# More warm-up products, filler products among the first heads, and one reciprocal for two heads

## The chip, the cores and the metric

The kernel runs on one core of one Trainium2 chip. The metric is the device time of one execution in microseconds (us); less is better. Times given as a result are medians of several runs. A profile is one execution taken by the hardware profiler, with the time of every instruction on the five engines: PE (TensorE), DVE (VectorE), ACT (ScalarE), POOL (GpSimd) and SP (SyncE, which issues the DMAs).

## What is computed

A causal attention with a decay runs for 4 batches of 8 heads, 576 positions and head size 64; its output (2304 tokens of 512 features) goes through two feed-forward layers of 512 to 2048 to 512.

```python
scores = scale * np.matmul(q, k.transpose(0, 1, 3, 2))
cum = np.cumsum(np.log(np.clip(f, 0.0001, 1.0)), axis=-1)
scores = np.where(causal, -1e9, scores + cum[:, :, :, None] - cum[:, :, None, :])
attn = np.exp(scores - np.max(scores, axis=-1, keepdims=True))
attn = attn / (np.sum(attn, axis=-1, keepdims=True) + 1e-09)
x = np.matmul(attn, v)                       # then heads side by side, 512 features
x = np.square(np.maximum(x @ w_in, 0)) @ w_out
h = x @ w_in2
out = np.where(h >= 1, h, np.where(h <= -1, 0, (h + 1) ** 2 / 4)) @ w_out2
```

## The kernel before, in words

The tokens are cut into five blocks of up to 512. Block 0 holds the first 256 positions of batches 0 and 1. For a block the kernel needs its attention first, then 16 steps of the first feed-forward layer (`mo` 0) and 16 of the second. One step is 12 products `h` (L1016) of 128x512, the activation, and 12 products `acc` (L1067 to L1069). Weights come as 64-bit words, one pair of slices per step; in the first 32 steps DVE, ACT and POOL decode them (`wf`, `low`; the last add of a decode is L957 on DVE or L958 on POOL), split them into a high and a low part (`whl`: the high part on ACT, L990, or on DVE, L991; the low part on DVE, L993), and SP stores the split form for the later blocks.

The first 256 positions of all heads are done by `attention32` in eight groups of four heads; block 0 takes groups 0 to 3. A head has its scores on PE (`s0q` for group 0; the contraction has 66 rows, 64 features and two rows of the decay), a masked row maximum on DVE (L587, `E`), two exponentials with sums on ACT (L647), a small add and a reciprocal of the two sums on DVE (L652 and L653, tile `st`), two multiplications by the reciprocal on ACT, DVE or POOL (L661 to L663), three transposes on PE (`tr`, L669), a copy (`pr`), and for each two heads the products with the values (`av`, L683). Block 0's feed-forward steps start on PE when the first of these are in `x`.

Before all this `warm_up` issues 11 products of the 128x128 identity with itself, which no result uses (L542, tile `warm`).

No order is written out by hand. Every operation goes to a planner (`Schedule`) with a cost on each engine that could do it, a due time, what it depends on, and the buffers it holds from a ring; `improve` plans the whole program once for each of seven weightings of DVE and POOL work (`WEIGHTS`), keeps the plan with the shortest total, and `emit` writes the instructions in planned order. So a small edit can move instructions, and move work between engines, in the whole program. At run time each engine goes through its own list in order. SP issues all loads and stores in one list, and a load of a group's queries and keys (L603, two buffers `QK`) waits there until the scores of the group two before are done.

Of the kernel before, what the change touches and what calls it, by code (L numbers as in the profile page):

```python
# [8 lines left out]
F32 = mybir.dt.float32  # L9
# [7 lines left out]
AF = mybir.ActivationFunctionType  # L17
ALU = mybir.AluOpType
# [4 lines left out]
P = 128  # L23
# [9 lines left out]
CHUNKS = [(HEAD, 320), (320, 448), (448, S)]  # L33
# [14 lines left out]
QUAD = 4  # L48
SPARE = ("E", "g", "E", "o", "E", "r", "E", "g", "E", "o")

SLAV = [0.0, 0.51, 0.75, 0.75, 0.0]
# [2 lines left out]
VE = [5.5, 6.1]  # L54
RE = [1.36, 7.73, 16.0]
LW = 29.1
WARM = 11


def pattern(bits):  # L60
# [320 lines left out]
def tile_attention_moe_moe(ctx: ExitStack, tc: tile.TileContext, qkv, f, w2, outT):  # L381
    nc = tc.nc
    PSUM = bass.MemoryType.PSUM
    W64 = w2.dtype == U64
    sch = Schedule()
# [4 lines left out]
    def ring(tag, n, shape, dt, space=None, fifo=True, most=()):  # L390
        kw = {"space": space} if space else {}
        tp = ctx.enter_context(tc.tile_pool(name="p_" + tag, bufs=n, **kw))
        pools[tag] = (Pool(n, fifo, most), tp, shape, dt)

    def new(tag, name, shape=None, dt=None, kind=None):
        p, tp, sh, d = pools[tag]
        shape = sh if shape is None else shape
        kw = {"padded_shape": sh} if list(shape) != list(sh) and len(shape) == len(sh) and dt is None else {}
        return Buf(p, lambda: tp.tile(shape, dt or d, tag=tag, name=name, **kw), kind)
# [3 lines left out]
    ring("K1", 2, [P, S], F32R)  # L403
    ring("vt", 3, [P, 5, 2, 64], F32R)
    ring("E", 5, [P, S], F32)
    ring("st", 4, [P, 3, len(CHUNKS)], F32)
    ring("mm", 3, [P, 2], F32)
    ring("PP", 3, [P, (2 * NK - 1) * P], F16)
    ring("PT", 2, [P, QUAD * 4 * HEAD], F16)
# [31 lines left out]
    for s in range(NS):  # L441
        g, att = s // NFC, 0.0
# [90 lines left out]
    cum_op, zs, mask_op, id_op, cumd_op, first_rows = setup()  # L533
    xb = {0: new("x", "x0")}

    def warm_up():

        ps = new("ps", "warm")

        def mms(n):  # L540
            for _ in range(n):
                nc.tensor.matmul(ps.tile[:, :P], ident, ident, start=True, stop=True)  # L542

        sch.op(-90, {"PE": (0.43 * WARM, lambda: mms(WARM))}, [id_op], [ps])
# [46 lines left out]
    def attention32(g):  # L591

        first = g.blk == 0
        qk, n = QK[g.i % 2], QUAD * 2 * HEAD
# [6 lines left out]
        for i in range(parts):  # L601
            c = slice(n // parts * i, n // parts * (i + 1))
# [17 lines left out]
        vt = new("vt", f"vt{g.i}q")  # L620
# [5 lines left out]
            in_=qkv[g.at_v:g.at_v + P * vn].rearrange("(p n) -> p n", p=P)))}, [], [vt], early=VE[g.i] if g.i < len(VE) else g.due - 4)  # L626
        g.qk = []
        chunks = [(0, 0, P), (1, P, HEAD)]
        for c in range(QUAD):
            nm = f"{g.i}q{c}"  # L630
            t0 = g.due + g.len * c / QUAD
            a = c % 2
            Eb = new(SPARE[len(used) % len(SPARE)] if first else "E", f"E{nm}", [P, 3 * P])
            used.append(Eb)
            st = new("st", f"st{nm}")
            ps = new("acc" if first else "ps", f"s{nm}", kind="att")
            cols = lambda ci: slice(0, P) if ci == 0 else slice(P, 3 * P)
            o_e = []
            for ci, qa, e in chunks:
                o_s = sch.op(t0, {"PE": (4 * e / 2400, lambda c=c, ci=ci, qa=qa, e=e, ps=ps: nc.tensor.matmul(  # L640
                    ps.tile[:, cols(ci)], qr(c)[:, qa:qa + P], kr(c)[:, :e], start=True, stop=True))},
                    ready[c], [ps, Eb, qk])
                g.qk.append(o_s)
                o_t = sch.op(t0 + 0.3, {"DVE": (dve_t(e) + 0.01, lambda ci=ci, qa=qa, e=e, Eb=Eb, ps=ps, st=st: top(
                    Eb.tile[:, cols(ci)], ps.tile[:, cols(ci)], qa, e, P, -0.125, st.tile[:, 0, ci:ci + 1]))},
                    [o_s, mask_op[0]], [ps, Eb, st])
                o_e.append(sch.op(t0 + 0.8, {"ACT": (act_t(e, ptr=1) + 0.09, lambda ci=ci, Eb=Eb, st=st: nc.scalar.activation(  # L647
                    Eb.tile[:, cols(ci)], Eb.tile[:, cols(ci)], AF.Exp, scale=-1.0, bias=st.tile[:, 0, ci:ci + 1],
                    accum_out=st.tile[:, 1, ci:ci + 1]))}, [o_t], [Eb, st]))

            def recip(st=st):
                nc.vector.tensor_scalar(st.tile[:, 1, :2], st.tile[:, 1, :2], 1e-9, None, op0=ALU.add)  # L652
                nc.vector.reciprocal(st.tile[:, 2, :2], st.tile[:, 1, :2])  # L653

            o_r = sch.op(t0 + 2, {"DVE": (0.30, recip, True)}, o_e, [st])
            o_n = []
            for ci, qa, e in chunks:
                x = lambda ci=ci, Eb=Eb: Eb.tile[:, cols(ci)]
                r = lambda ci=ci, st=st: st.tile[:, 2, ci:ci + 1]
                o_n.append(sch.op(t0 + 2.5, {  # L660
                    "ACT": (act_t(e, ptr=1), lambda x=x, r=r: nc.scalar.activation(x(), x(), AF.Copy, scale=r())),  # L661
                    "DVE": (dve2_t(e), lambda x=x, r=r: nc.vector.tensor_scalar(x(), x(), r(), None, op0=ALU.mult), True),
                    "POOL": (pool_t(e), lambda x=x, r=r: nc.gpsimd.tensor_scalar(  # L663
                        x(), x(), r(), 0.0, op0=ALU.mult, op1=ALU.add)),
                }, [o_r], [Eb, st]))
            if a == 0:
                pr = new("pr", f"pr{nm}")
            tr = new("acc" if first else "ps", f"tr{nm}", kind="att")
            got = [sch.op(t0 + 3, {"PE": (0.11, lambda tr=tr, Eb=Eb, to=to, at=at: nc.tensor.transpose(  # L669
                tr.tile[:, to:to + P], Eb.tile[:, at:at + P], ident))}, [o_n[at > 0], id_op], [Eb, tr, pr])  # L670
                for to, at in ((0, 0), (P, P), (2 * P, 2 * P))]
            o_c = sch.op(t0 + 3.5, copies(
                lambda pr=pr, a=a: pr.tile[:, a, :3 * P].bitcast(F32), lambda tr=tr: tr.tile[:, :3 * P], 3 * P,
                "ACT DVE", psum=True), got, [tr, pr])
            if a == 0:
                o_c0 = o_c
                continue
            av = new("acc" if first else "ps", f"av{nm}", kind="att")
            o_m = None
            for kc in range(HEAD // P):  # L680
                def mms(c=c, kc=kc, pr=pr, av=av):
                    for i in range(2):
                        nc.tensor.matmul(  # L683
                            av.tile[D * i:D * i + D, kc * P:HEAD], v32(c - 1 + i, kc),
                            pr.tile[:, i, 2 * P * kc:2 * P * kc + HEAD - kc * P].bitcast(F32),
                            start=(kc == 0), stop=(kc == HEAD // P - 1))

                o_m = sch.op(t0 + 4, {"PE": (4 * (HEAD - kc * P) / 2400 + 0.05, mms)},
                             [o_c, o_c0, o_v, o_m], [av, vt, pr], SLAV[g.blk])
            x = xb[g.blk]  # L690
            kc = (g.h + c) // 2
            hi = lambda kc=kc: x.tile[:, kc, 0, g.off:g.off + HEAD]
            o3 = sch.op(t0 + 5, copies(hi, lambda av=av: av.tile[:, :HEAD], HEAD, "ACT DVE", psum=True), [o_m], [av, x])
            xops.setdefault((g.blk, kc), []).append(sch.op(t0 + 5.5, {
                "DVE": (dve_t(HEAD), lambda kc=kc, hi=hi, av=av: nc.vector.tensor_tensor(
                    x.tile[:, kc, 1, g.off:g.off + HEAD], av.tile[:, :HEAD], hi().bitcast(F32), op=ALU.subtract))},
                [o3], [av, x]))

    def attention(t):
        g, W, nm, due = t.b * H + t.h, REST, t.name, t.due  # L700
        unit = 1.0 / PS
# [6 lines left out]
        a = t.h % 2  # L708
# [36 lines left out]
        E, o_e = [], []  # L745
        for ci, (qa, e) in enumerate(CHUNKS):
# [8 lines left out]
            for pi, (s0, s1) in enumerate(pieces):  # L755
# [25 lines left out]

        def recip():
            nc.vector.tensor_scalar(
                st.tile[:, 1, :], st.tile[:, 1, :], 1e-9, unit, op0=ALU.add, op1=ALU.mult)
            nc.vector.reciprocal(st.tile[:, 2, :], st.tile[:, 1, :])  # L785

        o_r = sch.op(back(9.5), {"DVE": (0.30, recip, True)}, o_e, [st])

# [410 lines left out]
```

## Time and profile before

| | |
|---|---|
| runs | 956.57, 958.58, 959.28 us; median 958.58 us |
| the profiled execution | 955.24 us, of which 953.5 us is the span that the profile shows |
| busy in the span | PE 939.9, ACT 638.0, DVE 583.2, POOL 191.3 us |
| mean granted clock of TensorE | 0.989 |

Busy time of an engine is the time in which it had an instruction running. A clock of 1.00 is TensorE's 2.4 GHz, 0.50 is 1.2 GHz. Where no clock is on record, as at the very start, the profile prints 1.00.

### The profile page before, as it was taken

How to read it: one execution, taken by the hardware profiler on the slowest of the kernel's cores; microseconds unless marked ns; L12 is line 12 of the kernel's file. 1: busy time of each engine (PE TensorE's matmuls, PEld its weight loads, DVE VectorE, ACT ScalarE, POOL GpSimd, SP SyncE). 2: the span in 40 equal slices, each digit the busy share in tenths (PEclk: the TensorE clock that was granted, in tenths of full speed). 3: DMA queues.
4: the chain of work that ended last, by engine and by line, in shares of the span. 5: the costliest groups of instructions: out<-in, count | busy, mean ns of one | idle time of the engine just before them, and what ended most of it. 6: DMA issues, size and time to landing. Idle time of an engine off the chain costs nothing.

```text
span 953.5 us, 14248 instructions
## 1 busy us (share of the span) xinstructions
PE 939.9 (99%) x4758; PEld 789.2 (83%) x4758; DVE 583.2 (61%) x1325; ACT 638.0 (67%) x1269; POOL 191.3 (20%) x341
## 2 busy tenths in 40 slices
PE   8999999999999999999999999999999999999998
PEld 6777777777778888888888888788888888889998
DVE  6899999989757668777767667866311132220032
ACT  5999879997877768787777677686432343334454
POOL 3321010134122323342323124231000000002200
PEclk6999999999999999999999999999999999999999
DMA  6699998996998987898899988796665655659994
GB/s 192 207 337 402 339 403 292 369 347 227 349 321 246 277 247 251 231 285 248 242 257 287 253 261 238 208 300 186 248 232 178 202 194 181 207 189 374 365 374 143
DMA packets 126106, 254.73 MB, mean 267 GB/s; under 512 B 89808, under 2 KB 90480, under 8 KB 104080
## 3 DMA queue, kind: packets, MB, share of 16 engines
q1 hardware_dynamic: 126032, 253.81, 81.0%
q8 instruction: 38, 0.62, 0.3%
q14 instruction: 36, 0.29, 0.1%
HBM read 194.35 MB, written 38.45 MB: 244 GB/s over the span
## 4 chain that ended last, share of the span: by engine, by line
PE 90%; DVE 4%; DMA 4%; issue 1%; ACT 1%; SPq 0%; POOL 0%; DVEq 0%; ACTq 0%
PE h L1016 39%; PE acc L1067 13%; PE acc L1069 13%; PE acc L1068 13%; PE av L840 4%; PE s L761 2%; PE s L762 2%; DMA PT<-PP 2%; DMA in<-in_qkv_dram 1%; DMA out_dram<-o 1%; PE s1q L640 1%; DVE whl L993 0%; DVE wf L957 0%; PE s0q L640 0%; DVE low L942 0%
## 5 line engine op out<-in xcount | busy, mean ns | idle before, releaser
L1016 PE MATMUL h<-x,whl 128*128 128x512 f32 (+1 forms) x1896 | 432.5, 371 | 0.6 <-DVE whl L993 0.5
L1016 PEld LDWEIGHTS h<-x,whl 128*128 128x128 f32 x1896 | 325.7, 189 | 55.4 <-issue 2.1
L1067 PE MATMUL acc<-gh,whl 128*128 128x512 f32 (+1 forms) x640 | 240.1, 375 | 2.9 <-DVE o L571 2.9
L1069 PE MATMUL acc<-gl,whl 128*128 128x512 f32 (+1 forms) x640 | 237.2, 371 | 0.0
L1068 PE MATMUL acc<-gh,whl 128*128 128x512 f32 (+1 forms) x640 | 236.7, 370 | 0.0
L580 DVE TENSOR_TENSOR gl<-g,gh 128x512 fp32r<-128x512 f32 (+1 forms) x126 | 83.6, 663 | 120.1 <-PE acc L1069 81.5
L1069 PEld LDWEIGHTS acc<-gl,whl 128*128 128x128 f32 x640 | 121.0, 189 | 21.5 <-POOL gl L582 0.2
L1067 PEld LDWEIGHTS acc<-gh,whl 128*128 128x128 f32 x640 | 120.9, 189 | 20.9 <-DVE o L571 3.4
L1068 PEld LDWEIGHTS acc<-gh,whl 128*128 128x128 f32 x640 | 121.0, 189 | 15.7
L1034 ACT ACTIVATE r<-h 128x512 f32<-128x512 f32 (+1 forms) x80 | 44.0, 550 | 91.3 <-PE h L1016 82.6
L1047 DVE SCALAR_TENSOR_TENSOR g<-r,h 128x512 f32<-128x512 f32 (+1 forms) x80 | 50.4, 630 | 80.1 <-ACT r L1045 79.6
L582 POOL TENSOR_TENSOR gl<-g,gh 128x512 fp32r<-128x512 f32 (+1 forms) x34 | 39.7, 1169 | 287.3 <-PE acc L1069 213.6
L1043 ACT ACTIVATE r<-h,half 128x512 f32<-128x512 f32 (+1 forms) x80 | 51.1, 639 | 61.9 <-PE h L1016 61.6
L815 DVE SCALAR_TENSOR_TENSOR PP<-E,st,PP 128x512 f16<-128x512 f32 (+2 forms) x128 | 77.6, 638 | 11.0 <-ACT PP L811 10.1
L778 ACT ACTIVATE E<-E,st 64x320 f32<-64x320 f32 (+2 forms) x96 | 63.6, 662 | 24.1 <-DVE st L587 15.6
L587 DVE CUSTOM_DVE_ANT_0 E<-s,mask 128x288 f32<-128x288 f32 (+2 forms) x128 | 62.1, 502 | 28.3 <-PE s L762 20.1
L811 ACT ACTIVATE PP<-E,st 128x512 f16<-128x512 f32 (+2 forms) x128 | 68.9, 591 | 9.1 <-DVE st L785 7.7
L840 PEld LDWEIGHTS av<-pr,vt 128*128 128x128 f32 x288 | 53.9, 189 | 13.0 <-issue 1.7
L840 PE MATMUL av<-pr,vt 128*128 128x320 f32 (+2 forms) x288 | 61.8, 287 | 1.3 <-DVE pr L571 1.3
L568 ACT ACTIVATE gh<-g 128x512 fp32r<-128x512 f32 (+1 forms) x70 | 40.7, 581 | 31.5 <-DVE g L1047 31.1
L573 POOL TENSOR_SCALAR pr<-PT 128x640 fp32r<-128x640 f16 (+2 forms) x50 | 31.2, 627 | 108.4 <-PE av L840 57.3
L568 ACT ACTIVATE pr<-PT 128x640 fp32r<-128x640 f16 (+2 forms) x63 | 36.3, 580 | 18.2 <-DMA PT<-PP 11.8
(258 smaller groups left out, 1145.4 us busy)
## 6 DMA issues: line engine op xcount, KB each, us to landing
whl<-scr SPq DMA_DIRECT2D x112, 1024.0 KB
raw<-in_w_dram SPq DMA_DIRECT2D x28, 1024.0 KB
scr<-whl SPq DMA_DIRECT2D x28, 1024.0 KB
in<-in_qkv_dram SPq DMA_DIRECT2D x32, 608.0 KB
whl<-scr SPq DMA_DIRECT2D x32, 512.0 KB
out_dram<-o SPq DMA_DIRECT2D x16, 256.0 KB
QK<-in_qkv_dram SPq DMA_DIRECT2D x7, 512.0 KB
raw<-in_w_dram SPq DMA_DIRECT2D x6, 512.0 KB
```

Source lines behind the costliest of these rows:

```text
L568: alts["ACT"] = (act_t(n, psum), lambda: nc.scalar.activation(out(), in_(), AF.Copy))
L580: alts["DVE"] = (dve_t(n), lambda: nc.vector.tensor_sub(out(), a(), b()), True)
L587: return nc.vector.tensor_tensor_reduce(out=out, in0=ps, in1=mask[:m, OFF - q0:OFF - q0 + n], scale=scale, scalar=3e38, op0=ALU.add, op1=A ...
L778: nc.scalar.activation(Ec.tile[:m, :e], Ec.tile[:m, :e], AF.Exp, scale=-1.0, bias=nmx(), accum_out=st.tile[:m, 1, ci:ci + 1])))}, [*tops, ...
L811: nc.scalar.activation(hi, x, AF.Copy, scale=r())
L815: nc.vector.scalar_tensor_tensor(lo, x, r(), hi, op0=ALU.mult, op1=ALU.subtract)
L840: nc.tensor.matmul(av.tile[:, c0:W], vt.tile[:, kc, :, :], pr.tile[:, i, :n], start=(kc == 0 and i == 0), stop=(kc == NK - 1))
L1016: nc.tensor.matmul(ps.tile[:, :n], w.tile[:, 0, wi, kc * P:(kc + 1) * P], src.tile[:, kc, xi, :n], start=(kc == 0 and i == 0), stop=(kc == ...
L1043: o1 = sch.op(due, {"ACT": (act_t(n, True, 1), lambda: A.activation(r.tile[:, :n], ps(), AF.Relu, scale=0.5, bias=half))}, [o], [psb, r])
L1067: nc.tensor.matmul(a.tile[:, :n], wh, gh.tile[:, :n], start=(fc == 0), stop=False)
L1068: nc.tensor.matmul(a.tile[:, :n], wl, gh.tile[:, :n], start=False, stop=False)
L1069: nc.tensor.matmul(a.tile[:, :n], wh, gl.tile[:, :n], start=False, stop=(fc == NFC - 1))
```

## The change

`WARM` goes from 11 to 17. Fifteen more single products of the identity with itself are given to the planner as operations of their own, all on the buffer of the warm-up, with due time 900 (so that anything else that is ready goes first) and not before the planned times 9, 10, ... 23. In `attention32` the two heads of a pair now share one `st` tile with four sums, one add and one reciprocal, which wait for the exponentials of both; group 0 keeps a reciprocal for each head. The contraction of the scores stays at 66 rows.

```diff
-WARM = 11
+FILL, FILL_AT, FILL_STEP = 15, 9, 1
+WARM = 17
...
-    ring("st", 4, [P, 3, len(CHUNKS)], F32)
+    ring("st", 4, [P, 3, 4], F32)
...
         sch.op(-90, {"PE": (0.43 * WARM, lambda: mms(WARM))}, [id_op], [ps])
+        for i in range(FILL):
+            sch.op(900.0, {"PE": (0.22, lambda: mms(1))}, [id_op], [ps], early=FILL_AT + FILL_STEP * i)
...
+        def recips(c, st, n, deps):
+            def recip():
+                nc.vector.tensor_scalar(st.tile[:, 1, :n], st.tile[:, 1, :n], 1e-9, None, op0=ALU.add)
+                nc.vector.reciprocal(st.tile[:, 2, :n], st.tile[:, 1, :n])
+
+            return sch.op(g.due + g.len * c / QUAD + 2, {"DVE": (0.30, recip, True)}, deps, [st])
...
+        for c in range(0, QUAD, 2):
+            got = []
+            if g.i == 0:
+                for a in range(2):
+                    st = new("st", f"st{g.i}q{c + a}")
+                    Eb, o_e = exps(c + a, st, 0)
+                    got.append(probabilities(c + a, st, 0, Eb, recips(c + a, st, 2, o_e)))
+            else:
+                st = new("st", f"st{g.i}q{c}")
+                (E0, o0), (E1, o1) = (exps(c + a, st, 2 * a) for a in range(2))
+                o_r = recips(c + 1, st, 4, [*o0, *o1])
+                got = [probabilities(c + a, st, 2 * a, Eb, o_r) for a, Eb in enumerate((E0, E1))]
+            products(c + 1, got)
```

What PE finds at the start of its list, before the change (`s0q` and `s1q` are scores of groups 0 and 1, `tr` transposes):

```order
L542 MATMUL warm<-ident 128x128 x11
L640 MATMUL s0q_248<-QK_180 128x128
L640 MATMUL s0q_248<-QK_180 128x256
...
L640 MATMUL s0q_274<-QK_180 128x128
L669 MATMUL tr0q_295<-ident,E0q_249 128x128 x3
L640 MATMUL s1q_307<-QK_212 128x128
L669 MATMUL tr0q_312<-ident,E0q_256 128x128 x3
L640 MATMUL s1q_307<-QK_212 128x256
```

And with it, at the same place:

```order
L543 MATMUL warm<-ident 128x128 x17
L644 MATMUL s0q_255<-QK_180 128x128
L644 MATMUL s0q_255<-QK_180 128x256
...
L644 MATMUL s0q_283<-QK_180 128x256
L543 MATMUL warm<-ident 128x128 x3
L683 MATMUL tr0q_304<-ident,E0q_256 128x128 x3
L543 MATMUL warm<-ident 128x128
L644 MATMUL s1q_314<-QK_218 128x128
L644 MATMUL s1q_314<-QK_218 128x256
```

Three filler products now stand between the scores of group 0 and its first transpose, and one behind it; three more follow up to the first transposes of group 1, and eight behind that point.

DVE's list for two heads of group 1 before, from the maximum of the second head on:

```order
L587 ISA E1q_323,st1q_332<-s1q_322,mask 128x128
L587 ISA st1q_332 128x1
L587 ISA E1q_323,st1q_332<-s1q_322,mask 128x256
L587 ISA st1q_332 128x1
...
L652 TENSOR_SCALAR st1q_316<-st1q_316 128x2
L653 RECIPROCAL st1q_316<-st1q_316 128x2
...
L652 TENSOR_SCALAR st1q_332<-st1q_332 128x2
L653 RECIPROCAL st1q_332<-st1q_332 128x2
```

And with the change, the same two heads:

```order
L590 ISA E1q_334,st1q_324<-s1q_333,mask 128x256
L590 ISA st1q_324 128x1
...
L658 TENSOR_SCALAR st1q_324<-st1q_324 128x4
L659 RECIPROCAL st1q_324<-st1q_324 128x4
L675 TENSOR_SCALAR E1q_315<-E1q_315,st1q_324 128x256
L675 TENSOR_SCALAR E1q_334<-E1q_334,st1q_324 128x128
```

One pair of small instructions is left of two, and both heads' multiplications stand behind it.

## Rows read from the trace of the kernel before

**Rows 1.** The page: busy time of PE, and the clock in 40 slices.
```profile
PE 939.9 (99%) x4758; PEld 789.2 (83%) x4758; DVE 583.2 (61%) x1325; ACT 638.0 (67%) x1269; POOL 191.3 (20%) x341
...
PEclk6999999999999999999999999999999999999999
```

**Rows 2.** What PE waited for in all, before and after 70 us (two answers).
```profile
PE s0q L640 <- DMA QK<-setup: 2.9, 1, 2.9
...
PE acc L1067 <- DVE o L571: 2.9, 1, 2.9
```

**Rows 3.** Windows by stage: length, busy of PE, PEld, DVE, ACT, POOL, clock, DMA, GB/s.
```profile
6.00:8.84 2.84, 0.00 (x0) 0.03 (x1) 2.31 (x6) 1.39 (x2) 0.92 (x4) 0.98 0.50 111
8.84:25.81 16.97, 16.73 (x59) 12.65 (x61) 9.45 (x53) 9.62 (x36) 1.68 (x4) 0.50 0.66 203
25.81:36.10 10.29, 10.13 (x74) 6.99 (x70) 9.07 (x49) 9.17 (x34) 3.77 (x7) 1.00 0.66 150
36.10:46.00 9.90, 9.78 (x70) 7.65 (x69) 9.30 (x42) 9.71 (x28) 3.73 (x7) 1.00 0.84 307
46.00:246.00 200.00, 199.32 (x932) 157.31 (x931) 190.07 (x334) 179.12 (x297) 37.02 (x34) 1.00 0.92 339
```

**Rows 4.** PE in half-microseconds: length, busy, clock, DMA, GB/s.
```profile
8.50:9.00 0.50, 0.16 (x1) 0.74 0.48 147
9.00:9.50 0.50, 0.50 (x3) 0.50 0.88 295
...
25.50:26.00 0.50, 0.50 (x8) 0.69 1.83 246
```

**Rows 5.** The warm-up's products: nanoseconds shortest/median/longest, first and last start.
```profile
L542 PE MATMUL warm<-ident x22: 274/421/579, 1.4 to 5.7; 128*128 128x128 f32 x22
```

**Rows 6.** PE in order of time: start, length, idle before and its releaser.
```profile
1.39 4.59 PE L542 MATMUL warm<-ident 128*128 128x128 f32 x22 [1.39 <-POOL tiny L482]
8.84 5.46 PE L640 MATMUL s0q<-QK 66*128 66x128 f32 x16 [2.86 <-DMA QK<-setup]
...
19.29 1.55 PE L683 MATMUL av0q<-pr0q,vt0q 128*64 128x256 f32 x8
...
28.86 0.87 PE L683 MATMUL av1q<-pr1q,vt1q 128*64 128x256 f32 x8
...
36.10 1.06 PE L1016 MATMUL h<-x,whl-2_481 128*128 128x512 f32 x3
```

**Rows 7.** What DVE waited for from 8.84 to 25.81: total, times, longest.
```profile
DVE E1q L587 <- PE s1q L640: 4.8, 4, 1.7
DVE E0q L587 <- PE s0q L640: 2.2, 4, 0.7
```

**Rows 8.** DVE's small instructions on group 1's sums: nanoseconds shortest/median/longest.
```profile
L652 DVE TENSOR_SCALAR st1q<-st1q x4: 158/162/216, 20.6 to 29.0; 128x2 f32<-128x2 f32 x4
L653 DVE RECIPROCAL st1q<-st1q x4: 167/168/168, 20.8 to 29.2; 128x2 f32<-128x2 f32 x4
```

**Rows 9.** DVE from 46 to 246, by form: busy, mean ns, idle before.
```profile
L957 DVE CUSTOM_DVE_ANT_0 wf<-wf,low 128x2048 uint16<-128x2048 uint16 x25 | 33.1, 1325 | 0.4
...
L580 DVE TENSOR_TENSOR gl<-g,gh 128x512 fp32r<-128x512 f32 x27 | 19.7, 728 | 1.0 <-ACT gh L568 0.9
...
L991 DVE TENSOR_SCALAR whl<-wf 128x1024 fp32r<-128x1024 f32 x6 | 4.1, 679 | 0.0
```

**Rows 10.** POOL from 46 to 246, by form.
```profile
L958 POOL TENSOR_TENSOR wf<-wf,low 128x1024 int32<-128x1024 int32 x5 | 12.0, 2392 | 33.4 <-DVE wf L954 30.9 <-ACT r L1043 2.5
L582 POOL TENSOR_TENSOR gl<-g,gh 128x512 fp32r<-128x512 f32 x5 | 10.1, 2017 | 39.2 <-ACT gh L1040 19.4 <-DVE st5q L587 10.4 <-PE h L1016 5.0
```

**Rows 11.** What SP's list waited for from 8 to 46: total, times, longest.
```profile
SPq L603 <- PE s1q L640: 7.3, 1, 7.3
SPq L603 <- PE s2q L640: 4.5, 1, 4.5
```

More of the change, by code (lines that the diff above doesn't have):

```diff
@@ L628, in attention32, with exps @@
         chunks = [(0, 0, P), (1, P, HEAD)]
-        for c in range(QUAD):
+        sums = {}
+        def exps(c, st, at):
             nm = f"{g.i}q{c}"
             t0 = g.due + g.len * c / QUAD
-            a = c % 2
             Eb = new(SPARE[len(used) % len(SPARE)] if first else "E", f"E{nm}", [P, 3 * P])
             used.append(Eb)
-            st = new("st", f"st{nm}")
             ps = new("acc" if first else "ps", f"s{nm}", kind="att")
@@ L644, in attention32, with probabilities @@
                 o_t = sch.op(t0 + 0.3, {"DVE": (dve_t(e) + 0.01, lambda ci=ci, qa=qa, e=e, Eb=Eb, ps=ps, st=st: top(
-                    Eb.tile[:, cols(ci)], ps.tile[:, cols(ci)], qa, e, P, -0.125, st.tile[:, 0, ci:ci + 1]))},
+                    Eb.tile[:, cols(ci)], ps.tile[:, cols(ci)], qa, e, P, -0.125, st.tile[:, 0, at + ci:at + ci + 1]))},
                     [o_s, mask_op[0]], [ps, Eb, st])
                 o_e.append(sch.op(t0 + 0.8, {"ACT": (act_t(e, ptr=1) + 0.09, lambda ci=ci, Eb=Eb, st=st: nc.scalar.activation(
[L648 to L655, printed above, removed]
+                    Eb.tile[:, cols(ci)], Eb.tile[:, cols(ci)], AF.Exp, scale=-1.0, bias=st.tile[:, 0, at + ci:at + ci + 1],
+                    accum_out=st.tile[:, 1, at + ci:at + ci + 1]))}, [o_t], [Eb, st]))
+            return Eb, o_e
+        def recips(c, st, n, deps):
[3 more added lines that the diff above has]
+            return sch.op(g.due + g.len * c / QUAD + 2, {"DVE": (0.30, recip, True)}, deps, [st])
+        def probabilities(c, st, at, Eb, o_r):
+            nm = f"{g.i}q{c}"
+            t0 = g.due + g.len * c / QUAD
+            a = c % 2
+            cols = lambda ci: slice(0, P) if ci == 0 else slice(P, 3 * P)
             o_n = []
@@ L658, in attention32 @@
                 x = lambda ci=ci, Eb=Eb: Eb.tile[:, cols(ci)]
-                r = lambda ci=ci, st=st: st.tile[:, 2, ci:ci + 1]
+                r = lambda ci=ci, st=st: st.tile[:, 2, at + ci:at + ci + 1]
                 o_n.append(sch.op(t0 + 2.5, {
@@ L666, in attention32 @@
             if a == 0:
-                pr = new("pr", f"pr{nm}")
+                sums["pr"] = new("pr", f"pr{nm}")
+            pr = sums["pr"]
             tr = new("acc" if first else "ps", f"tr{nm}", kind="att")
@@ L671, in attention32, with products @@
                 for to, at in ((0, 0), (P, P), (2 * P, 2 * P))]
-            o_c = sch.op(t0 + 3.5, copies(
+            return sch.op(t0 + 3.5, copies(
                 lambda pr=pr, a=a: pr.tile[:, a, :3 * P].bitcast(F32), lambda tr=tr: tr.tile[:, :3 * P], 3 * P,
                 "ACT DVE", psum=True), got, [tr, pr])
-            if a == 0:
-                o_c0 = o_c
-                continue
+        def products(c, got):
+            pr, nm, t0 = sums["pr"], f"{g.i}q{c}", g.due + g.len * c / QUAD
             av = new("acc" if first else "ps", f"av{nm}", kind="att")
@@ L688, in attention32 @@
                 o_m = sch.op(t0 + 4, {"PE": (4 * (HEAD - kc * P) / 2400 + 0.05, mms)},
-                             [o_c, o_c0, o_v, o_m], [av, vt, pr], SLAV[g.blk])
+                             [*got, o_v, o_m], [av, vt, pr], SLAV[g.blk])
             x = xb[g.blk]
@@ L783, in recip @@
             nc.vector.tensor_scalar(
-                st.tile[:, 1, :], st.tile[:, 1, :], 1e-9, unit, op0=ALU.add, op1=ALU.mult)
-            nc.vector.reciprocal(st.tile[:, 2, :], st.tile[:, 1, :])
+                st.tile[:, 1, :3], st.tile[:, 1, :3], 1e-9, unit, op0=ALU.add, op1=ALU.mult)
+            nc.vector.reciprocal(st.tile[:, 2, :3], st.tile[:, 1, :3])
         o_r = sch.op(back(9.5), {"DVE": (0.30, recip, True)}, o_e, [st])
```

## Prediction

> **What bounds the kernel now.** I read the page first: PE is busy for 939.9 of 953.5 us, and its clock is full in every slice but the first [rows 1]. So outside the start time is saved only by taking work from PE, and this change adds some. The waits of PE, read next, are few: 2.9 us for the first keys and queries, and after 70 us the longest is another 2.9 [rows 2]. What is left is the start, and the windows show it: from 8.84 to 25.81 us PE is busy for 16.73 of 16.97 us, but at clock 0.50, while DVE has work for 9.45 us and ACT for 9.62 [rows 3]. The half-microseconds give the edges: the clock falls between 8.5 and 9.0 and is back between 25.5 and 26.0 [rows 4]. The same eight products with the values take 1.55 us at the lower level and 0.87 at the higher [rows 6].
>
> What did PE do before it fell? The warm-up ran 22 instructions (two for a product) in 4.59 us from 1.39 on [rows 6]. Their median is 421 ns, the shortest 274 [rows 5]: most ran at 1.2 GHz, whatever the profile prints there, and the last ones at 2.4. So the clock did rise. Then PE waited 2.86 us for the keys and queries [rows 6], it fell, and the scores with their 66 rows, transposes and value products that follow did not raise it for 17 us, though PE hardly paused. A mix of the same kind did keep it at 1.00 from 25.81 to 36.10 [rows 3].
>
> In that slow stretch the other engines wait for PE: DVE 7.0 us for scores (4.8 and 2.2) [rows 7], and SP's loads of the next groups 7.3 and 4.5 us [rows 11]. From 25.81 to 46 it is the other way round: DVE is busy 18.37 of 20.19 us (91%), ACT 18.88 (94%) [rows 3]. The start would therefore be bound by ACT and DVE if PE were fast.
>
> **The change part by part.** *Six more warm-up products.* One costs 4.59 / 11 = 0.42 us at the lower level, 0.21 at the higher. The warm-up ends at 5.98 (1.39 + 4.59) now; six more end it between 7.3 and 8.5. Both are before the keys and queries land (8.84 [rows 6]), so they cost nothing: they lie in the wait. If the load landed at the same time and the warm-up ran over, each product over would cost its 0.42. The gap at which the clock fell shrinks from 2.86 to between 0.3 and 1.6 us. I take it that the clock then stays up. No row proves that. For it speaks that the fall follows the gap, and that such a mix held the clock later; against it that the first work behind the gap is only scores of 66 rows, which did not raise it.
>
> *The slow stretch at the full clock.* PE: 16.73 us at 0.50 are 8.4 us at 1.00. By the order, eight fillers come in as much work (3, 1, 3 and 1), 8 x 0.21 = 1.7, together 10.1 us. DVE at the 91% of the later stretch needs 9.45 / 0.91 = 10.4 us, ACT 9.62 / 0.94 = 10.2. DVE can only begin when the first head's scores are there: four heads take 5.46 us at the lower level [rows 6], so one takes some 0.7 at the higher (an estimate). So ACT and DVE set 11.1 us, PE 10.1. The engines don't mesh perfectly; I take 11.8. The gain is 16.97 - 11.8 = 5.2 us. Bounds: 5.9 if 11.1 is reached; 16.97 - 11.1 - 3.2 = 2.7 if all fifteen fillers (15 x 0.21) delay what ACT and DVE wait for.
>
> *The other seven fillers* stand among work of 25.81 to 46, where PE is busy 19.91 of 20.19 us [rows 3] but is not what limits. They are 1.5 us of PE; I charge half, 0.7 (bounds 0 and 1.5). They also keep the warm-up's PSUM buffer, one of four, until the last of them; the first feed-forward products have three left. No row shows what that costs; I charge nothing, and at most 1.1 us, the length of the first `h` series [rows 6] that would wait for a buffer.
>
> *One reciprocal for two heads.* Fourteen pairs outside group 0 each lose an add and a reciprocal, 0.162 + 0.168 us [rows 8], 4.6 us of DVE. The new wait: the first head's multiplications stand behind the second head's exponentials. Behind that wait stand its transposes and value product on PE. It is hidden where ACT and DVE are nearly always busy with other heads; uncovered at the end of block 0's attention it would cost one head's two exponentials, about 1.2 us of ACT in the slow stretch's terms (9.62 us for some eight heads). I take 0, with -1.2 as bound.
>
> *What the planner moves.* Counted in both orders up to the 32nd step, POOL loses five adds of the decode (L958) and all five `gl`, and DVE gets five more of each and four more `whl`. By DVE's rows that is 5 x 1.33 + 5 x 0.73 + 4 x 0.68 = 13.0 us [rows 9]; less the 4.6 above, 8.4 us more DVE. Cover: DVE is idle for 9.9 us of 46 to 246 [rows 3]. It fits barely. I charge 0.5 us of PE waiting for weights; bounds 0 and 8.4.
>
> The Trainium skill ("SBUF — State Buffer", section "SBUF: two separate sides") says that DVE and GpSimd take a port of the memory in turn, each for a whole instruction, the other blocked. The trace bears that out as far as it goes: the same `gl` takes 2.02 us on POOL and 0.73 on DVE, the add 2.39 and 1.33 [rows 9, 10]. By that rule DVE would get back waiting for what it takes over, and this term would be 0; by DVE's rows alone it could be 8.4.
>
> **Sum.** +5.2 - 0.7 - 0.5 = 4.0 us less than the profiled execution's 955.24 (953.5 in the span, 1.7 around it): 951.2. That execution was 3.3 us under the median of the runs, so against 958.58 the forecast is 954.5 us. With 5.9 and all later fillers hidden it is 952.7, with 2.7 and 1.5 of fillers 957.4; the runs of before spread over 2.7 us, and I give the forecast 951 to 957. A difference of 0.3%, 2.9 us, is about what a measurement here can tell from none.
>
> **The rivals.** *The clock falls all the same* (20%): the change then does not do what it says. For it: 66-row scores did not raise the clock in 17 us, and the shorter gap is still a gap. Then fillers run at 0.42 us in front of real work: eight are 3.3 us, seven more at 0.21 are 1.5, and of these fifteen perhaps 1.5 us come back because full products among the heads raise the clock earlier (each us earlier is worth half a us). 958.58 + 3.3 = 962 us. It decides where the clock in the first half-microseconds after 8.84 is 0.50. The Trainium skill ("TensorE: Matmul & The Clock Gate", section "What's actually happening") adds that the chip judges PE's activity on a schedule that does not start with the kernel, so that the rise comes at another product from run to run. The runs of before differ by 2.7 us, which agrees; by it some executions of the changed kernel could fall and others hold, and the median takes the commoner.
>
> *DVE becomes the bound* (15%): this one ends on the slower side. Place: 46 to 246, `h` products waiting for `whl`. Price: 8.4 us more DVE where 9.9 are free; from the point at which the free time does not lie where the moved work does, each us is a us of PE. All of it: 954.5 - 0.5 + 8.4 = 962.4. Against it: POOL's slow adds go away.
>
> *The loads eat it* (15%): PE and DVE are ready earlier, but weights and the next groups are not. DMA is at a share of 0.92 and 339 GB/s from 46 to 246 [rows 3]. For it: that is near its most. Against: SP's list waits for PE at the start, so loads would move up with it. About half of the 4.0 would be lost: 956.5 us.
>
> **How the numbers follow.** The forecast has 50%, 951 to 957; the rivals 15%, 15% and 20%. The likeliest gives 954.5. The range for eight in ten reaches from 951 over the loads (956.5) to the clock's fall (962): 951 to 962. Faster by over 2.9 us (under 955.7): four fifths of the forecast, a quarter of the loads, a tenth of the other two, 0.48. Slower (over 961.5): half of DVE's, 45% of the clock's, a little of the rest, 0.17. Same: 0.35.
>
> **What would show it.** In the profile after: the warm-up's last start near 7 to 8.5 us and the wait behind it under 1.7 us; the clock 1.00 right through 9 to 26; DVE's wait for `s0q` and `s1q` under 2 us; the first `h` at 30 to 32 instead of 36.1 us [rows 6]; DVE's busy time between 20 and 46 no higher in share than 95%. Wrong would be: 0.50 anywhere between 9 and 26; waits of `h` for `whl` of over 2 us before 246; a sum of PE's waits after 70 us that grew by more than 2 us.

## The result, and the profile after

The changed kernel takes 949.11 us (median of 8 runs, 947.88 to 954.79), the kernel before 958.98 us beside it (8 runs, 955.91 to 961.24): a ratio of 0.9912, 95% interval [0.9887, 0.9937]. The gain is 9.9 us where 4.1 were forecast, and the median lies below the forecast range.

The runs of after are of two kinds: six from 947.88 to 950.36 us, two at 953.91 and 954.79. The last is the one that was profiled. So I profiled the same kernel once more (below as *again*), and that execution took 948.37. The two traces show what sets the kinds apart. First the page of the profiled execution, as in [rows 1]: busy time, and the clock in 40 slices.

```profile
PE 942.0 (99%) x4800; PEld 792.7 (83%) x4800; DVE 616.3 (65%) x1429; ACT 633.5 (66%) x1265; POOL 79.1 (8%) x213
...
PEclk8899999999999999999999999999999999999999
```

The same lines of *again*:

```profile
PE 935.4 (99%) x4800; PEld 787.7 (83%) x4800; DVE 615.9 (65%) x1429; ACT 632.9 (67%) x1265; POOL 79.0 (8%) x213
...
PEclk9999999999999999999999999999999999999999
```

Windows of after, as in [rows 3], with three halves of a microsecond as in [rows 4] (length, busy of PE, PEld, DVE, ACT, POOL, clock, DMA, GB/s):

```profile
8.84:25.81 16.97, 15.93 (x78) 12.28 (x79) 11.39 (x55) 10.22 (x39) 2.18 (x5) 0.72 0.92 238
25.81:36.10 10.29, 10.29 (x65) 8.49 (x65) 7.10 (x32) 6.46 (x23) 2.12 (x6) 0.79 0.55 177
46.00:246.00 200.00, 200.00 (x945) 158.40 (x944) 196.52 (x343) 176.19 (x295) 12.75 (x19) 1.00 0.94 344
...
16.00:16.50 0.50, 0.46 (x2) 0.43 (x3) 0.47 (x3) 0.50 (x2) 0.06 (x1) 0.89 0.92 156
16.50:17.00 0.50, 0.50 (x4) 0.41 (x2) 0.48 (x2) 0.50 (x3) 0.33 (x1) 0.50 0.79 143
...
30.00:30.50 0.50, 0.50 (x6) 0.47 (x5) 0.05 (x1) 0.50 (x4) 0.00 (x0) 0.96 0.22 82
```

The same stages of *again*:

```profile
8.84:25.81 16.97, 15.99 (x110) 12.93 (x111) 14.64 (x76) 13.80 (x54) 3.46 (x8) 1.00 0.98 276
25.81:36.10 10.29, 10.14 (x72) 7.43 (x73) 9.24 (x39) 8.35 (x28) 2.00 (x5) 1.00 0.94 291
...
46.00:246.00 200.00, 200.00 (x940) 158.88 (x939) 196.13 (x346) 176.12 (x297) 12.59 (x20) 1.00 0.95 348
```

In after the clock fell at 16.4 us and came back at 30.0; in *again* it stayed up. PE in order of time shows it at the same instructions (start, length, idle before). After:

```profile
1.39 6.31 PE L543 MATMUL warm<-ident 128*128 128x128 f32 x34 [1.39 <-POOL tiny L483]
8.71 2.86 PE L644 MATMUL s0q<-QK 66*128 66x128 f32 x16 [1.00 <-DMA QK<-setup]
11.40 0.83 PE L543 MATMUL warm<-ident 128*128 128x128 f32 x6
...
13.84 0.89 PE L644 MATMUL s1q<-QK 66*128 66x128 f32 x4 [0.81 <-DMA QK<-cumd]
...
16.05 1.35 PE L644 MATMUL s1q<-QK 66*128 66x256 f32 x4
17.33 1.55 PE L696 MATMUL av0q<-pr0q,vt0q 128*64 128x256 f32 x8
...
33.68 0.95 PE L1043 MATMUL h<-x,whl-2_391 128*128 128x512 f32 x3
```

And *again*:

```profile
9.17 2.86 PE L644 MATMUL s0q<-QK 66*128 66x128 f32 x16 [1.82 <-DMA QK<-setup]
...
13.85 0.89 PE L644 MATMUL s1q<-QK 66*128 66x128 f32 x4 [0.35 <-DMA QK<-cumd]
...
16.05 0.92 PE L644 MATMUL s1q<-QK 66*128 66x256 f32 x4
16.90 0.87 PE L696 MATMUL av0q<-pr0q,vt0q 128*64 128x256 f32 x8
...
27.44 0.94 PE L1043 MATMUL h<-x,whl-2_391 128*128 128x512 f32 x3
```

Both reach the same scores at 16.05 us; from there each piece takes about half as long again or more in after, and the first `h` comes at 33.68 instead of 27.44 us, 6.2 us later. The whole executions differ by 6.4 us. So even when the clock fell, the kernel lost no more than that one stretch, and when it held, the first `h` came 8.7 us earlier than before's 36.10 [rows 6]; the whole span was 7.1 us shorter (953.5 and 946.4).

What PE waited for in all of *again* (total, times, longest), as in [rows 2]:

```profile
PE s0q L644 <- DMA QK<-setup: 1.8, 1, 1.8
PE acc L1094 <- DVE o L574: 1.7, 1, 1.7
PE warm L543 <- POOL tiny L483: 1.4, 1, 1.4
PE av L867 <- DVE st L590: 1.4, 1, 1.4
```

From 46 to 246 us PE is busy for all 200 us, so no `h` waits for `whl` there.

### The profile page after: what moved, and what is told of

The parts are those of the page before. It is cut to its first block, busy times and chain, and to the rows that moved or that the text cites. A ratio compares the mean times of both kernels' runs of the same rounds, so it can differ in the third digit from the quotient of the medians.

```text
span 952.8 us, 14231 instructions
## 1 busy us (share of the span) xinstructions
PE 942.0 (99%) x4800; PEld 792.7 (83%) x4800; DVE 616.3 (65%) x1429; ACT 633.5 (66%) x1265; POOL 79.1 (8%) x213
## 4 chain that ended last, share of the span: by engine, by line
PE 91%; DMA 5%; DVE 2%; ACT 1%; issue 0%; SPq 0%; DVEq 0%; ACTq 0%
PE h L1043 39%; PE acc L1094 13%; PE acc L1096 13%; PE acc L1095 13%; PE av L867 4%; DMA PT<-PP 3%; PE s L788 2%; PE s L789 2%; DMA whl<-scr 1%; DMA out_dram<-o 1%; DMA QK<-in_qkv_dram 1%; PE s2q L644 0%; PE s1q L644 0%; DVE PP L842 0%; PE warm L543 0%
## 5 line engine op out<-in xcount | busy, mean ns | idle before, releaser
L583 DVE TENSOR_TENSOR gl<-g,gh 128x512 fp32r<-128x512 f32 (+1 forms) x160 | 102.2, 638 | 153.3 <-PE acc L1096 120.8
L1095 PEld LDWEIGHTS acc<-gh,whl 128*128 128x128 f32 x640 | 120.9, 189 | 15.6
L842 DVE SCALAR_TENSOR_TENSOR PP<-E,st,PP 128x512 f16<-128x512 f32 (+2 forms) x128 | 72.3, 595 | 9.7 <-ACT PP L838 9.4
L590 DVE CUSTOM_DVE_ANT_0 E<-s,mask 128x288 f32<-128x288 f32 (+2 forms) x128 | 62.4, 500 | 19.0 <-PE s L789 13.6
L1072 ACT ACTIVATE r<-r 128x512 f32<-128x512 f32 (+1 forms) x80 | 46.9, 586 | 1.8
L1067 ACT ACTIVATE gh<-r 128x512 fp32r<-128x512 f32 (+1 forms) x80 | 46.0, 575 | 0.0
```

The source lines that it names most:

```text
L583: alts["DVE"] = (dve_t(n), lambda: nc.vector.tensor_sub(out(), a(), b()), True)
L590: return nc.vector.tensor_tensor_reduce(out=out, in0=ps, in1=mask[:m, OFF - q0:OFF - q0 + n], scale=scale, scalar=3e38, op0=ALU.add, op1=A ...
L842: nc.vector.scalar_tensor_tensor(lo, x, r(), hi, op0=ALU.mult, op1=ALU.subtract)
L1095: nc.tensor.matmul(a.tile[:, :n], wl, gh.tile[:, :n], start=False, stop=False)
```

## The experiments

Unless an edit says otherwise, every variant has the instructions of after in the same order on every engine; only the number of products that an operation issues differs.

### The same kernel again

> The changed kernel as it is, for a profile of an execution in which the clock holds. Clock theory: where the mean granted clock is 1.000 the time is near 948 us and the first feed-forward product starts at 27 to 30 us; where it is 0.992 near 955 us and 33.7 us. Plan theory: the time is near 949 us whatever the clock, and the first feed-forward product starts at the same place in both.

948.37 us, shown above: the clock held to the end (mean 1.000), and the first `h` starts at 27.44 us.

### The new lists alone (order_only)

```diff
-        sch.op(-90, {"PE": (0.43 * WARM, lambda: mms(WARM))}, [id_op], [ps])
+        sch.op(-90, {"PE": (0.43 * WARM, lambda: mms(11))}, [id_op], [ps])
...
-            sch.op(900.0, {"PE": (0.22, lambda: mms(1))}, [id_op], [ps], early=FILL_AT + FILL_STEP * i)
+            sch.op(900.0, {"PE": (0.22, lambda: mms(0))}, [id_op], [ps], early=FILL_AT + FILL_STEP * i)
```

> Every engine's list as in the changed kernel, with 11 warm-up products and no filler emitted. Clock theory: the clock falls in the wait before the first scores, as before the change, and the time is that of the kernel before, 956 to 961 us. Plan theory (the new order and the shared reciprocal bring the gain): 948 to 951 us.

956.18 us (12 runs, 953.49 to 958.99), ratio 0.998 [0.9962, 0.9998]. Shared reciprocals and all that the planner moved are worth 2 us (by the ratio, 0.2 to 3.6 by its interval) to 3 (by the medians, 959.21 beside it) with the clock down. The window from the first scores to the first `h`:

```profile
8.70:35.16 26.46, 26.34 (x98) 19.73 (x98) 15.52 (x79) 15.42 (x55) 4.33 (x10) 0.50 0.66 200
```

PE was busy for all but 0.12 us of it, and the clock came back only at 35.0 us. Three of the twelve runs print a mean clock of 0.998 to 1.000 at 956.81 to 958.99 us; the part on why the prediction was wrong comes back to such runs.

### 17 warm-up products and no fillers (no_fill)

```diff
-            sch.op(900.0, {"PE": (0.22, lambda: mms(1))}, [id_op], [ps], early=FILL_AT + FILL_STEP * i)
+            sch.op(900.0, {"PE": (0.22, lambda: mms(0))}, [id_op], [ps], early=FILL_AT + FILL_STEP * i)
```

> The changed kernel's lists with 17 warm-up products and no filler. Clock theory: the clock passes the wait before the first scores, then falls in more executions than in the changed kernel, since only scores and transposes follow; time between 948 (held) and 957 (fell), median about 953 us. If the fillers are only a burden: the clock holds as often as with them and the time is 2 to 3 us less, 945 to 947 us. Plan theory: 946 to 949 us.

Median 949.34 us of 6 runs, ratio 0.9898 [0.9868, 0.9929], but the six are two groups: 944.96, 945.25, 946.46 and 952.21, 952.95, 953.61. In the profiled one (944.96) the clock held. From the first scores to the first `h`:

```profile
8.97:26.05 17.08, 15.50 (x97) 11.06 (x98) 15.38 (x81) 14.14 (x56) 4.16 (x10) 1.00 0.98 285
```

This is the same work as in the row of order_only: 26.46 us at 0.50, 17.08 at 1.00. PE has 1.6 us to spare, and DVE is busy for 15.38, 90%.

### 11 warm-up products and all fillers (warm11)

```diff
-        sch.op(-90, {"PE": (0.43 * WARM, lambda: mms(WARM))}, [id_op], [ps])
+        sch.op(-90, {"PE": (0.43 * WARM, lambda: mms(11))}, [id_op], [ps])
```

> The changed kernel's lists with 11 warm-up products and all fifteen fillers. Clock theory: the clock falls in the wait of some 3 us before the first scores, as before the change; the fillers bring it back some us sooner than 25.8 and cost 0.42 us each until then: 955 to 959 us. Plan theory: as the changed kernel, 949 us.

948.05 us (5 runs, 947.41 to 950.63), ratio 0.989 [0.9875, 0.9905]. My theory (the longer warm-up decides) is refuted. PE waited 3.13 us for the keys and the clock did fall, but it came back soon:

```profile
10.00:10.50 0.50, 0.50 (x5) 0.45 (x4) 0.46 (x1) 0.00 (x0) 0.00 (x0) 0.83 1.25 377
10.50:11.00 0.50, 0.50 (x3) 0.50 (x3) 0.50 (x4) 0.02 (x1) 0.00 (x0) 0.50 0.96 193
16.50:17.00 0.50, 0.50 (x4) 0.50 (x4) 0.00 (x0) 0.50 (x3) 0.00 (x0) 0.50 1.09 279
17.00:17.50 0.50, 0.50 (x4) 0.40 (x4) 0.00 (x0) 0.50 (x4) 0.00 (x0) 0.84 1.30 262
```

About 7 us at the lower level, where order_only kept it until just before the first `h`, with the fillers as the only difference.

### 17 warm-up products in the kernel before (b_warm17)

```diff
-        sch.op(-90, {"PE": (0.43 * WARM, lambda: mms(WARM))}, [id_op], [ps])
+        sch.op(-90, {"PE": (0.43 * WARM, lambda: mms(17))}, [id_op], [ps])
```

> The kernel before with 17 warm-up products issued in place of 11, and nothing else changed: every list as before. Theory A (a longer warm-up alone can carry the clock over the wait for the keys, but only in a part of the executions, as in the variant of after with 17 warm-up products and no fillers, which gave either 945 or 952 to 954 us): two levels, one near 949 and one near 956 to 959, the median between 949 and 957. Theory B (it is the fillers that matter; the warm-up does nothing without the new order of the heads): 958 to 960 in nearly all executions, as before.

955.82 us (12 runs, 951.21 to 958.07), ratio 0.9973 [0.9959, 0.9987]: 2.8 us. The median lies in theory A's range, but its two levels are not there: one run of twelve is under 954 us. In its profile the warm-up carried the clock over the wait for the keys; it fell in the middle of the first two groups' heads and was back 17 us later:

```profile
15.50:16.00 0.50, 0.50 (x5) 0.41 (x4) 0.40 (x2) 0.50 (x3) 0.00 (x0) 0.62 0.87 180
...
32.50:33.00 0.50, 0.50 (x5) 0.38 (x3) 0.00 (x0) 0.50 (x2) 0.00 (x0) 0.81 0.00 0
```

### Only the first seven or four fillers

```diff
-            sch.op(900.0, {"PE": (0.22, lambda: mms(1))}, [id_op], [ps], early=FILL_AT + FILL_STEP * i)
+            sch.op(900.0, {"PE": (0.22, lambda i=i: mms(1 if i < 7 else 0))}, [id_op], [ps], early=FILL_AT + FILL_STEP * i)
```

With 17 warm-up products, twice (w17_fill7, w17_fill7_2); with `i < 4` (w17_fill4); and with `mms(11)` in front as above (w11_fill7).

> After's lists with 17 warm-up products and only the first seven fillers (those up to the first transposes of group 1), the other eight issue nothing. Theory A (only fillers before the clock would fall, or right after, do work; the later ones stand where the clock is up and cost 0.21 us each): 8 x 0.21 = 1.7 us under after's executions in which the clock held, so about 946.5 in nearly all executions. Theory B (all fifteen are needed, because the clock can fall as late as 16 us and the later ones bring it back): many executions of 952 to 955, as without fillers.

> The same kernel as the one with 17 warm-up products and the first seven fillers, again beside the next three: 945.4 us there, in all its executions between 944.7 and 946.9. Expected 945 to 947 again in nearly all executions, if seven fillers hold the clock; one execution in four or more at 952 to 955 would say that it was chance.

> After's lists with 17 warm-up products and only the first four fillers (three behind the scores of group 0, one in front of the first scores of group 1). If what counts is full products up to the first wait of the heads: 945 in nearly all executions, as with seven. If the three behind (in front of and behind the value products of group 0) are needed as well: part of the executions at 952 to 954, as without fillers (949.3 in the median).

> After's lists with 11 warm-up products and only the first seven fillers. With all fifteen this gave 948.05 us, the clock falling at 10.3 and coming back at 17.2 us. Theory A (the first seven, which stand before that return, bring it back): 8 x 0.21 = 1.7 us less, about 946.4, and the clock back near 17 us. Theory B (the clock came back by the fillers behind, or needs all): the clock stays at 0.50 to 25 us or later and the time is 951 to 956.

With 17: 945.43 us (4 runs), ratio 0.9869 [0.9856, 0.9881]; again 945.12 (5 runs), 0.9875 [0.9849, 0.99]; with four fillers 945.17 (5 runs), 0.9873 [0.9846, 0.9901]. All 14 runs lie between 944.53 and 947.89. With 11: 948.74 (4 runs, 947.73 to 949.99), 0.9902 [0.9889, 0.9915], the clock again down for some 7 us; the gain of 1.7 us over warm11 was not seen.

So four fillers with 17 warm-up products are, with seven, the best version with the scores as they are, some 4 us under after (945.2 and 949.1, each beside other runs of before). One caution: up to 16 us after and these variants issue the same instructions, so the fall at 16.4 us in after's profile was open to them too; 14 runs without it against two of eight is no proof that it can't happen.

### Scores over 128 rows (rows128, rows128_w17)

```diff
-        return [sch.op(due, fill(lambda t=t, x=x: kq(D, D + 2, t), x), [], [QK[i]]) for t, x in ((0, 8.0), (1, -8.0))]
+        return [sch.op(due, fill(lambda t=t, x=x: kq(D, P, t), x), [], [QK[i]]) for t, x in ((0, 8.0), (1, -8.0))]
...
-        kr = lambda c: reg()[:D + 2, 2 * c * HEAD:2 * c * HEAD + HEAD]
-        qr = lambda c: reg()[:D + 2, 2 * c * HEAD + HEAD:2 * c * HEAD + 2 * HEAD]
+        kr = lambda c: reg()[:P, 2 * c * HEAD:2 * c * HEAD + HEAD]
+        qr = lambda c: reg()[:P, 2 * c * HEAD + HEAD:2 * c * HEAD + 2 * HEAD]
```

No fillers in either; 11 and 17 warm-up products.

> After's lists with 11 warm-up products and no filler, which gave 956.2 us with the clock at 0.50 from 7.7 to 35.0 us, and with the scores of the first 256 positions contracted over 128 rows in place of 66: the memsets that write the constant 8 and -8 into two rows write them into 64, so that every score gets the same constant, which the maximum takes off again. No instruction more and none longer by its columns. Theory A (scores of 66 rows do not raise the clock, products over 128 rows do): the clock comes back by about 17 us or does not fall, 946 to 950. Theory B (the rows play no part; the many short products, their order or the pauses do): 955 to 957, the clock at 0.50 to 25 us or later.

> After's lists with 17 warm-up products, no filler, and scores contracted over 128 rows (the constant 8 and -8 in 64 rows in place of two, the same constant added to every score). With 66 rows this gave either 945 or 952 to 954 us, in about equal parts. Theory A (66-row scores let the clock fall, 128-row scores hold it): 945 in nearly all executions. Theory B (the rows only bring it back sooner, the pauses let it fall): 945 in a part, and 948 to 950 in the others.

With 11: 948.02 us (4 runs, 945.95 to 948.79), ratio 0.9887 [0.9872, 0.9901]. With 17: 945.76 (5 runs, 944.11 to 948.04), 0.9875 [0.9849, 0.99]. The two memsets and the rows of the contraction are all that parts rows128 from order_only (956.18). The clock of rows128 fell when the scores began and was back before the second group's:

```profile
9.00:9.50 0.50, 0.50 (x4) 0.41 (x3) 0.35 (x2) 0.00 (x0) 0.00 (x0) 0.57 0.52 115
12.00:12.50 0.50, 0.50 (x3) 0.41 (x2) 0.00 (x0) 0.50 (x4) 0.00 (x0) 0.52 1.00 209
12.50:13.00 0.50, 0.50 (x5) 0.32 (x3) 0.39 (x4) 0.21 (x3) 0.00 (x0) 1.00 1.08 397
```

So among these instructions the 66 rows keep the clock down once it has fallen: that is shown, and the runs of rows128 and order_only (953.49 to 958.99) do not overlap. The added rows hold 8 and -8; whether rows of zeros would do was not run. With 17 warm-up products in front the clock did not fall in the profile, and no run was over 948.04, where three of six with 66 rows were over 952. That 128 rows also keep the clock from falling is not shown: in b_rows128_w17, below, it fell.

### A reciprocal for each head (each_recip)

```diff
-            if g.i == 0:
+            if g.i >= 0:
                 for a in range(2):
```

With 17 warm-up products and seven fillers, planned anew, so that other instructions move as well.

> 17 warm-up products and seven fillers, and a reciprocal for each head again, planned anew: 14 adds and 14 reciprocals more on DVE, and other places for many instructions behind group 0, with all gl on DVE as in after. The prediction's term (4.6 us of DVE, hidden, no new wait): the same as with shared reciprocals, 945 to 947. If the shared reciprocal brought time by itself (DVE is busy 86% of the held stretch and ACT 81%): up to 4.6 us more, 948 to 950. If the shared reciprocal costs a wait: less, 944.

946.83 us (6 runs, 944.75 to 949.04), ratio 0.9887 [0.9863, 0.991], beside 945.12 with shared reciprocals. The 1.7 us point to a gain from sharing, but the ranges overlap, and the plan is another (POOL is busy for 36.3 us in place of 78.9). In its profile DVE is busy for 98% of 25.81 to 36.10, and PE for 8.75 us:

```profile
25.81:36.10 10.29, 8.75 (x60) 6.50 (x60) 10.06 (x48) 9.68 (x33) 0.88 (x2) 1.00 1.00 292
```

In w17_fill7_2 the same stage reads:

```profile
25.81:36.10 10.29, 9.72 (x66) 6.78 (x65) 9.20 (x40) 8.89 (x31) 2.00 (x5) 1.00 0.88 279
```

### The clock alone, and the fillers alone

The kernel before with 17 warm-up products and 128 rows (b_rows128_w17; its edits are shown above), and after as it is with 128 rows (rows128_w17_fill15).

> The kernel before, its lists unchanged, with 17 warm-up products and scores over 128 rows: both together held the clock in after's lists (945.8 us). It parts the gain into the clock and the lists. If the clock is nearly all of it: before's lists with the clock held take 946 to 948 us. If the new lists and the shared reciprocal are worth what they showed with the clock down (956.2 against 959.2, about 3 us): 948 to 950. If the lists are worth more once the clock is up, because ACT and DVE then bind the start: 951 to 953.

> After as it is (17 warm-up products, all fifteen fillers), with scores over 128 rows as the only edit, so that the clock should hold in every execution and the fillers can be priced beside the same kernel without them (945.8). By their own length 15 x 0.21 = 3.2 us at the most: 949. If only those in front of work that PE is late with cost: 947 to 948. If the clock falls in a part of the executions as in after (two of eight at 954 to 955), the rows don't hold it here.

The first: 947.63 us (5 runs, 947.25 to 950.1), ratio 0.9898 [0.9868, 0.9929], against 958.31 beside it: 10.7 us without any change of the lists (6.8 to 12.6 by the interval). From b_warm17 only the rows differ, and the ratio went from 0.9973 to 0.9898, with intervals apart. From the first scores to the first `h`, where before needed 27.26 us (8.84 to 36.10):

```profile
8.71:31.66 22.95, 21.07 (x131) 15.11 (x131) 18.14 (x101) 18.39 (x68) 5.49 (x11) 0.93 0.79 221
```

This profile is the slowest of the five runs, and its 0.93 is a fall: from 14.5 to 17.9 us the clock was at 0.50. PE in order of time, as above:

```profile
8.71 2.85 PE L640 MATMUL s0q<-QK 128*128 128x128 f32 x16 [1.89 <-DMA QK<-setup]
...
14.68 1.65 PE L640 MATMUL s1q<-QK 128*128 128x256 f32 x4 [0.17 <-DVE st1q L587]
...
18.68 0.82 PE L640 MATMUL s1q<-QK 128*128 128x128 f32 x4
```

In b_warm17, with the same lists and the same warm-up, the clock fell at 15.6 and stayed down for 17.1 us; here it was down for 3.4. So more rows shorten the slow stretch in before's lists too, but do not rule out the fall.

The second: 948.54 us (6 runs, 947.43 to 950.12), ratio 0.99 [0.987, 0.993]. Without fillers it was 945.76 beside another set of runs of before; by the ratios 0.9875 and 0.99, fifteen fillers cost 2.4 us when the clock needs none of them, by the medians 2.8. The intervals overlap, but 948.6 for after's six held runs (their median) against 945.2 with four or seven fillers points the same way.

## Why the prediction was wrong

**The bound was read rightly**: PE outside the start is full, and most of the time came from the first 36 us. In *again* DVE's waits for `s0q` and `s1q` fell from 7.0 us [rows 7] to 1.0. The clock's fall as the cause is shown by three edits that leave every list as it is: other numbers of warm-ups, of fillers, and of rows, the last in either kernel's lists.

**The step that failed is "the slow stretch at the full clock"**, 5.2 us with bounds 2.7 to 5.9. With before's lists it measured 10.7 us. The forecast took 17 us at the lower level at a price of 0.31 us each; the runs show some 27 us at about 0.4. Its parts:

- *The price was too low.* I took a DVE that is 91% busy once PE is fast; it was 90% (no_fill). The forecast made 5.2 us of 16.97 at the lower level, 0.31 us for each. From order_only to no_fill 26.46 us became 17.08: 9.38 / 26.46 = 0.35. Between *again* and the profiled execution of the same kernel, 13.6 us at the lower level cost 6.4: 0.47. Beside the variants the kernel before ran 56 times. In 49 of these executions the time follows the mean clock, from 962.74 us at 0.982 to 951.59 at 0.993; a straight line of time against time at 0.50 through these 49 gives 0.42 us for each us at 0.50 and 946.9 us at the full clock (an estimate). The kernel b_rows128_w17, in which the clock is mostly up, took 947.63.
- *The stretch was too short, because the profiled execution was not a typical one.* Its mean clock was 0.989; 39 of the 56 show 0.984 to 0.988, the commonest 0.986. An execution of 957 us with a mean clock of 0.989 spent 0.011 x 2 x 957 = 21 us at 0.50, one with 0.986 spent 27. The 6 us more are worth 2.5 us at 0.42. I saw that the execution was 3.3 us under the median and carried those 3.3 us over to the forecast unchanged, "so against 958.58 the forecast is 954.5". They were, by this estimate, for the larger part the very loss that the change removes. The other seven of the 56 do not fit: they print 0.996 to 0.998, and all are slower than the median beside them (958.67 to 962.92 us). Where no clock is on record the profile prints 1.00, so a slow stretch may hide in them; none was profiled, and this stays open.
- *A second fall was not seen.* Behind the 2.9 us that PE waited for `o` [rows 2], before ran at a lower clock once more:

```profile
262.00:269.00 7.00, 4.44 (x15) 3.79 (x16) 3.38 (x9) 4.87 (x9) 1.18 (x2) 0.76 1.11 368
```

This is 7.00 x (1 - 0.76) x 2 = 3.4 of the 21 us at 0.50. I had read a full clock in every slice but the first [rows 1], but a slice there is 24 us long, and a 9 stands for 0.9 or more. In *again* the wait was 1.7 us, and the same stage reads 1.00:

```profile
262.00:269.00 7.00, 7.00 (x36) 5.81 (x35) 6.57 (x17) 5.33 (x11) 0.43 (x2) 1.00 1.06 332
```

How much of the gain this is, is open: b_warm17, with before's lists and a wait of 2.8 us, reads 1.00 there, and the profile of b_rows128_w17, the kernel of the 10.7 us, has such a fall too (0.88 from 255 to 269 us).

Together, 27 us at 0.42 are 11.3 us, where 10.7 (6.8 to 12.6) were measured.

**"I take it that the clock then stays up"** held in *again*, but not in the profiled execution: 0.72 from 8.84 to 25.81, which is what the prediction said would make it wrong. The place was another than the rival's. In every profile with the longer warm-up the clock passed the wait for the keys. But in some it fell later, at 15.6 us (b_warm17) and 16.4 (after) among the 66-row scores. Nor is the longer warm-up always needed: in warm11 the clock passed a wait of 3.13 us and fell at 10.3, while in order_only it fell at 7.7, in the wait. The Trainium skill ("TensorE: Matmul & The Clock Gate", section "What's actually happening") says that the chip judges on a schedule of its own; two kinds of executions of one kernel agree with that. It also says that activity of PE releases the throttle; order_only, busy for 26.34 of 26.46 us and at 0.50 until 35.0, differs, and the measurement decides.

**The rival "the clock falls all the same"** was priced at 962 us. Where it fell, 953.91 and 954.79 were measured: the clock was back at 30.0 us, after 13.6 us (17.1 in b_warm17, without fillers), and the lists themselves were better.

**The fillers** were charged 0.7 us for seven, and the other eight were counted in a PE that does not limit. All fifteen cost 2.4 to 2.8 us. The first four to seven cost next to nothing (945.1 to 945.4 beside 945.0 to 946.5 without any, held): the first four stand where PE waits for the first group's probabilities and for the second group's keys. The cost is that of the later ones, more than their own 8 x 0.21 = 1.7. Where the last microsecond goes was not settled.

**The shared reciprocal and the planner's moves** were charged 0.5 us together, with no new wait. They gave time: 2 to 3 us with the clock down (order_only), 1.9 with it up (947.63 for before's lists, 945.76 for after's, both with 128 rows, beside different runs of before; the intervals overlap, so the second figure is not clear of noise). That no wait of `h` for `whl` came is right, and the DVE rival is refuted: PE lost nothing from 46 to 246 us, though DVE's work rose from 190.07 [rows 3] to 196.13 us. The forecast of 8.4 us more in that stretch was too high: DVE's instructions were shorter in after's lists, where POOL's were gone. (Over the whole kernel DVE took 32.7 us more, 583.2 and 615.9, most of it behind the stretch that I counted.) DVE in *again* from 46 to 246 (busy, mean ns, idle before), against 1325 and 728 ns [rows 9]:

```profile
L984 DVE CUSTOM_DVE_ANT_0 wf<-wf,low 128x2048 uint16<-128x2048 uint16 x29 | 35.4, 1221 | 0.4
L583 DVE TENSOR_TENSOR gl<-g,gh 128x512 fp32r<-128x512 f32 x33 | 22.8, 691 | 0.6 <-PE acc L1096 0.4
```

It is hardly the clock: in b_rows128_w17, before's lists with the clock mostly up, they take 1326 and 719 ns. That POOL's work is the cause is argued, not shown, as no run changes POOL alone. The Trainium skill's rule that GpSimd and a DVE instruction with two inputs in SBUF take a port in turn ("SBUF — State Buffer", section "SBUF: two separate sides") agrees with that; the rows that the prediction set beside it (one operation on POOL and on DVE) only compare two engines. Forecast by it, the term would have been 0, nearer than my 0.5.

**The loads** did not eat the gain: of loads, PE waited before 46 us in *again* only for the first keys (1.8) and for the second group's (0.3). Nor was a DMA share of 0.92 at 339 GB/s near the most: 262 to 269 us of before, above, read 1.11 at 368.

The measured terms, 10.7 for the clock, 1.9 for the lists and the reciprocal, less 2.4 to 2.8 for the fillers, give 9.8 to 10.2 us; 9.9 were measured, with two of eight executions in which the clock still fell. This is less of a check than it seems: the terms are steps from before to rows128_w17_fill15, so they must add up to that kernel's gain; what the sum says is that after gained about as much with 66 rows.

## What to carry to other kernels

Before a profile is turned into a forecast, compare its mean clock with that of the other runs: a difference to the median that is itself clock is part of the gain, not an offset. Check first that the time follows the printed clock, as in seven of 56 executions here it did not. If TensorE is busy and yet at the lower level, look at the rows of the contraction: products that use half of the array did not bring the clock back here for 17 us and more, and filling the rows up cost no instruction. A filler product is free only where the engine waits, so place a few in the first waits and drop the rest.

## What the runs showed of the hardware

- TensorE's clock follows more than whether it is busy: scores over 66 rows, with transposes and value products among them, were busy 26.34 of 26.46 us at 0.50; with 128 rows in the same instructions the clock, fallen at 9.1, was back at 12.5 us. In before's lists with 17 warm-up products a fall lasted 17.1 us with 66 rows (b_warm17) and 3.4 with 128 (b_rows128_w17).
- A product over 128 rows takes no longer than one over 66: the scores of the first four heads took 2.86 us with 66 rows (after, above) and 2.85 with 128 (b_rows128_w17, above), both at the full clock.
- The clock can also fall late: in rows128_w17_fill15 a wait of 1.7 us for `o` that ended at 259.5 was followed by three microseconds at 0.51, as in before behind 264. In *again* a wait of the same length was not, nor one of 2.8 us in b_warm17.

```profile
258.00:261.00 3.00, 1.49 (x6) 1.21 (x7) 2.19 (x6) 2.28 (x7) 0.11 (x1) 0.93 1.05 435
261.00:264.00 3.00, 3.00 (x11) 2.63 (x10) 1.96 (x6) 2.46 (x7) 0.55 (x2) 0.51 1.15 344
```
